# An attention and two-layer kernel: the second layer's low weight bits by ScalarE, one softmax moved, eight constant products fewer

## The chip, the cores and the metric

The kernel runs on one core of one Trainium2 chip. The metric is the device time of one launch in microseconds (us). TensorE (PE in the profile) multiplies matrices into PSUM, VectorE (DVE), ScalarE (ACT) and GpSimd (POOL) work on vectors, and SyncE (SP) issues the transfers. Each engine runs its own instructions in the order in which they were issued to it, and waits on semaphores for the others.

## The reference

Windowed attention is followed by two matrix products with an activation between them:

```python
# q, k, v: (8, 8, 576, 64); w_in (512, 2048) and w_out (2048, 512) are float64
scores = scale * np.matmul(q, k.transpose(0, 1, 3, 2))
# heads 0-3: the last 32 positions; heads 4-7: every 4th of the last 128
scores = np.where(masks[None, :, :, :], scores, -1000000000.0)
attn = np.exp(scores - np.max(scores, axis=-1, keepdims=True))
attn = attn / (np.sum(attn, axis=-1, keepdims=True) + 1e-09)
x = np.matmul(attn, v)           # then (4608, 512): tokens by heads
h = x @ w_in
g = np.where(h >= 1, h, np.where(h <= -1, 0.0, (h + 1) ** 2 / 4.0))
return (g @ w_out).astype(np.float32)
```

## The kernel before

Attention of 8 batches of 8 heads yields 9 blocks of 512 tokens. The two layers go through 9 x 16 steps (t, f): block t of tokens, chunk f of 128 hidden channels. In step s TensorE runs `layer1` of step s (12 products, tiles `h`, L404), then `layer2` of step s - 2 (12 products into the four banks `acc`, L440). Pieces of attention of later heads are hung between these halves by `place` and `run(u)`: scores (`s`, L208), transposes (`t`, L331), products with the values (`o`, L366). TensorE's order is the order of the code, written out by hand, and so is SyncE's. The order on VectorE, ScalarE and GpSimd is set by a scheduler from the dependences, from the place in the code, from `high_priority` and from `issue_after`, which puts what is issued inside it behind a given instruction.

Exact products need each float32 operand in two parts, a rounded copy and its remainder. After `layer1`, L418 clamps `h` (DVE), L421 squares (ACT), L423 takes the maximum (DVE), L424 writes the rounded copy `gh` (ACT), and L427 the remainder `gl` (DVE). `layer2` needs both. `h` has two PSUM banks, so `layer1` of step s also waits for `gh` and `gl` of step s - 2.

The weights come as float64 words, 32 chunks: `wi0` to `wi15`, `wo0` to `wo15`. `weights` turns one into two parts: L116 scales the high word into `m` (ACT, three buffers for all chunks), the top three bits of the low word are cut out (for `wi` by a byte read and a scaled copy on ACT, L122; for `wo` by a shift on DVE, L124), L127 merges both (DVE), L132 writes the rounded copy (ACT), L133 the remainder (POOL). `layer1` and `layer2` wait for L133. Chunks wo0 and wi3 are prepared ahead of step 0, then wo s and wi s + 3 from step s on, behind a mark of step s - 2.

The second batch's heads 8 to 15 run during the first steps. `scores_pair` masks the scores and takes row maxima on DVE (L182, tile `c8` for head 8). `softmax` for heads 8, 9, 10, 12 and 14 is done in one piece (`whole`): POOL subtracts the maximum (L297), ACT takes the exponential of the tile (L298), DVE sums the rows (L299); head 11 takes six exponentials (L256). Then ACT adds a small constant (L290), DVE inverts (L291), POOL multiplies (L292). Only then may TensorE transpose `c8` (tiles `t8_0`, `t8_4`), which stands between `layer2` of step 0 and `layer1` of step 3; `t9` follows that `layer1`, then come `layer2` of step 1, the values product `o8`, step 4, `t10`. All the `s`, `t` and `o` tiles take turns in two PSUM banks (`att`), so `t10_0` waits until the first half of `o8` has been copied out (L350 on ACT, L351 on DVE), and `t10_4` until the second half has.

`spin` issues products of a constant that nothing uses: 14 of them stand ahead of `layer1` of step 2.

Of the kernel before, what the change touches and what calls it, by code (L numbers as in the profile page):

```python
# [26 lines left out]
U8 = mybir.dt.uint8  # L27
AF = mybir.ActivationFunctionType
ALU = mybir.AluOpType

B, H, S, D = 8, 8, 576, 64
# [14 lines left out]
def body(ctx, tc, q, k, q2, k2, v, mask, eye, w_in, w_out, out):  # L46
    nc = tc.nc
# [22 lines left out]
    def load_pair(n):  # L70

        if 0 < n < H:
            qr, kr = borrow(f"qr{n}")[:, :S], borrow(f"kr{n}")[:, :KPAD]
        else:
            tags = ("qs", "kk") if n % 4 else ("qr", "kr")
            qr = pool.tile([128, S], F32, tag=tags[0], name=f"qr{n}")
            kr = pool.tile([128, KPAD + 32], F32, tag=tags[1], name=f"kr{n}")[:, :KPAD]
        nc.sync.dma_start(out=qr, in_=q[n // 2])
        nc.sync.dma_start(out=kr, in_=k[n // 2])
        for j in range(2):  # L80
            r = slice(64 * j, 64 * j + 64)
            heads[n + j] = dict(qs=qr[r], ks=kr[r])
# [18 lines left out]
    wi, wo, raws = {}, {}, {}  # L101
# [7 lines left out]
    def weights(f, w, name):  # L109

        raw = raws.pop((name, f))
        words = raw.rearrange("p (n x) -> p n x", x=2)
        low, high = words[:, :, 0], words[:, :, 1]
        m = pool.tile([128, DM], U32, tag="m", name=f"{name}_m{f}", bufs=3)

        nc.scalar.activation(  # L116
            out=m.bitcast(F32), in_=high.bitcast(F32), func=AF.Prelu, scale=2.0**-112, alpha=2.0**32
        )
        if name == "wi":

            top = raw.bitcast(U8).rearrange("p (n x) -> p n x", x=8)[:, :, 3]
            nc.scalar.activation(out=low, in_=top, func=AF.Copy, scale=1.0 / 32, bias=-31.0 / 64)  # L122
        else:
            nc.vector.tensor_scalar(  # L124
                out=low, in0=low, scalar1=29, scalar2=None, op0=ALU.logical_shift_right
            )
        nc.vector.scalar_tensor_tensor(  # L127
            out=m, in0=m, scalar=3, in1=low, op0=ALU.logical_shift_left, op1=ALU.bitwise_or
        )
        mf = m.bitcast(F32)  # L130
        w[f] = pool.tile([128, 2, DM], F32R, tag=f"{name}{f}", name=f"{name}{f}")
        nc.scalar.copy(out=w[f][:, 0], in_=mf)  # L132
        nc.gpsimd.tensor_tensor(out=w[f][:, 1], in0=mf, in1=w[f][:, 0].bitcast(F32), op=ALU.subtract)  # L133
# [27 lines left out]
    def spin(times, bank):  # L161

        half = half_t.broadcast_to([128, 128])
        for _ in range(times):
            PE.matmul(out=bank[:, :128], lhsT=half, rhs=half, start=True, stop=True)  # L165
# [117 lines left out]
    def softmax(n):  # L283
        c, st = heads[n]["c"], heads[n]["st"]
        if n in (8, 9, 10, 12, 14):
            whole(n)
        else:
            for t in range(NQ):
                exp(n, t)
        nc.scalar.activation(out=st[:, 1], in_=st[:, 1], func=AF.Copy, bias=EPS)  # L290
        nc.vector.reciprocal(out=st[:, 2], in_=st[:, 1])  # L291
        nc.gpsimd.tensor_tensor(out=c, in0=c, in1=spread(st[:, 2]), op=ALU.mult)  # L292
# [43 lines left out]
    last = {}  # L336
    xt = {}

    def xtile(t):
        if t not in xt:  # L340
            xt[t] = (
                pool.tile([128, NC, TOK], F32R, tag="xh", name=f"xh{t}", bufs=3),
                pool.tile([128, NC, TOK], F32R, tag="xl", name=f"xl{t}", bufs=3),
            )
        return xt[t]
# [51 lines left out]
    def layer1(t, f, cs=range(NC), bank=("h", 2)):  # L397
        xh, xl = xtile(t)
        if cs[0] == 0 and (t, f) not in hps:
            hps[t, f] = ps.tile([128, TOK], F32, tag=bank[0], name=f"h{t}_{f}", bufs=bank[1])  # L400
        hp = hps[t, f]
        terms = [(w, x, c) for c in cs for w, x in ((0, xh), (1, xh), (0, xl))]
        for i, (w, x, c) in enumerate(terms):
            PE.matmul(  # L404
                out=hp,
                lhsT=wi[f][:, w, 128 * c : 128 * c + 128],
                rhs=x[:, c],
                start=c == 0 and i == 0,
                stop=c == NC - 1 and i == len(terms) - 1,
            )  # L410
        if cs[-1] < NC - 1:
            return
        del hps[t, f]
        y = pool.tile([128, TOK], F32, tag="y", name=f"y{t}_{f}")
        gh = pool.tile([128, TOK], F32R, tag="gh", name=f"gh{t}_{f}", bufs=2)
        gl = pool.tile([128, TOK], F32R, tag="gl", name=f"gl{t}_{f}", bufs=2)
        with tc.high_priority(offset=60):
            nc.vector.tensor_scalar(  # L418
                out=y, in0=hp, scalar1=-1.0, scalar2=1.0, op0=ALU.max, op1=ALU.min
            )  # L420
            nc.scalar.activation(out=y, in_=y, func=AF.Square, bias=half_t, scale=0.5)  # L421

            activated = nc.vector.tensor_tensor(out=hp, in0=hp, in1=y, op=ALU.max)  # L423
            copied = nc.scalar.copy(out=gh, in_=hp)  # L424
            if t == 0:
                last["g", f] = copied, activated
            nc.vector.tensor_tensor(out=gl, in0=hp, in1=gh.bitcast(F32), op=ALU.subtract)  # L427
        gs[t, f] = gh, gl

    acc = {}  # L430
# [31 lines left out]
    def after_pair(n):  # L462
        softmax(n)
        softmax(n + 1)
        if n + 4 < native:
            load_pair(n + 4)
        elif n + 4 == native:
            load(native)
        else:
            split(native)  # L470
            load(native + 1)
# [70 lines left out]
    def early_values(n):  # L542
        with tc.high_priority(offset=150):
            values(n)
# [14 lines left out]
    with tc.manual_schedule(engines={mybir.EngineType.PE, mybir.EngineType.SP}):  # L559
        pair(0)  # L560
        pair(2)
        pair(4)
        pair(6)
        hps[0, 0] = ps.tile([128, TOK], F32, tag="h", name="h0_0", bufs=2)
        early_transposes(0)
        load_values(8)
        fetch(1, w_out, "wo")
        fetch(4, w_in, "wi")
        load_pair(10)
        fetch(2, w_out, "wo")  # L570
        fetch(5, w_in, "wi")
        fetch(3, w_out, "wo")
        for f in range(6, 9):
            fetch(f, w_in, "wi")
            fetch(f - 2, w_out, "wo")
        early_values(0)
        early_transposes(2)
        early_values(2)
        first = marks()
        spin(10, hps[0, 0])  # L580
        early_transposes(4)
        spin(3, hps[0, 0])
        early_transposes(6)
        behind(first, ("wi", 0), ("wi", 1))
        early_values(4)
        second = marks()
        layer1(0, 0, range(2))
        early_values(6)
        third = marks()
        behind(second, ("wi", 2))  # L590
        layer1(0, 1, range(2))
        scores_pair(H, 0, 4)
        scores_pair(H, 4, NQ)
        for f in range(9, 14):
            fetch(f, w_in, "wi")
            fetch(f - 2, w_out, "wo")
        with tc.issue_after(third[0].ins), tc.issue_after(third[1].ins):
            after_pair(H)
        behind(third, ("wo", 0), ("wi", 3))
        l2 = 0  # L600
        steps = [(t, f) for t in range(NT) for f in range(NF)]
        lag = 2
        for s in range(len(steps) + lag):
            if s == 3:
                for f, src, name in ((12, w_out, "wo"), (13, w_out, "wo"), (14, w_in, "wi")):
                    fetch(f, src, name)
                for f, src, name in ((14, w_out, "wo"), (15, w_in, "wi"), (15, w_out, "wo")):
                    fetch(f, src, name)
            if 0 < s < NF:
                todo = [("wo", s)]  # L610
                if s + 3 < NF:
                    todo.append(("wi", s + 3))
                behind(last["g", max(s - 2, 0)], *todo)
            if s == 2:
                acc[0] = ps.tile([128, DM], F32, tag="acc0", name="acc0_0")
                spin(14, acc[0])
            if s < 2:
                layer1(*steps[s], range(2, NC))
            elif s < len(steps):
                layer1(*steps[s])  # L620
            run(2 * s)
            while l2 <= s - lag and l2 < len(steps):
                layer2(*steps[l2])
                l2 += 1
            run(2 * s + 1)
        assert not slots
# [63 lines left out]
```

## Time and profile before

| | us |
|---|---|
| median of 3 runs | 925.8 (925.31 to 926.72) |
| the profiled execution | 924.65 |
| its span in the trace | 922.9 |
| PE, DVE, ACT, POOL busy | 905.3, 683.9, 487.3, 239.8 |

The profiled execution is 1.75 us longer than its span and 1.15 us below the median. Times in rows of the timeline are from the span's start. A row gives start, length, engine, line, operation, the tile written and the tiles read with buffer numbers left out, and in brackets how long the engine had idled and which instruction ended that. TensorE's float32 products are recorded as two instructions where operands are float32, so that 14 constant products are 28 rows.

### The profile page before, as it was taken

The page shows a single profiled execution, that of the slowest core. Times are in us where ns is not written, and L with a number is a line of the kernel's source. Part 1 is how long each engine was busy: PE and PEld are TensorE (multiplying, and loading weights), DVE is VectorE, ACT ScalarE, POOL GpSimd, SP SyncE. Part 2 cuts the span into 40 slices and gives each one's busy share as a digit, 9 for nine tenths or more (in the row PEclk, how much of TensorE's full clock was granted, in tenths as well). Part 3 has the DMA queues.
Part 4 walks back from the last instruction along what each step waited for, and adds up shares of the span by engine and source line. Part 5 has one row for each costly group of instructions (what it writes and reads, how often), then busy time and mean ns, then how long its engine had stood idle before and what let it go on. Part 6 is the DMA issues. An engine that isn't in the chain of part 4 may idle for free.

```text
span 922.9 us, 14426 instructions
## 1 busy us (share of the span) xinstructions
PE 905.3 (98%) x4886; PEld 742.5 (80%) x4886; DVE 683.9 (74%) x1982; ACT 487.3 (53%) x1336; POOL 239.8 (26%) x155
## 2 busy tenths in 40 slices
PE   7889999999999999999999999999999999999998
PEld 6677788888888888888888888888888888888886
DVE  6898898888888888788887888888888643334333
ACT  6778865555555556555555665555555322222222
POOL 4566453222223222222222322222222000000000
PEclk9999999999999999999999999999999999999999
DMA  9981003221232223112322223222321010001001
GB/s 350 407 311 45 1 27 103 84 58 57 70 116 71 70 71 107 51 57 69 116 71 71 71 61 103 67 70 71 116 71 44 1 46 1 1 1 47 0 1 47
DMA packets 31018, 73.87 MB, mean 80 GB/s; under 512 B 3520, under 2 KB 3808, under 8 KB 30944
## 3 DMA queue, kind: packets, MB, share of 16 engines
q1 hardware_dynamic: 30944, 72.94, 24.4%
q8 instruction: 39, 0.64, 0.3%
q14 instruction: 35, 0.29, 0.1%
HBM read 63.49 MB, written 9.44 MB: 79 GB/s over the span
## 4 chain that ended last, share of the span: by engine, by line
PE 91%; DMA 3%; DVE 3%; ACT 2%; issue 1%; POOL 1%; DVEq 0%; POOLq 0%; SPq 0%; ACTq 0%
PE acc L440 42%; PE h L404 40%; PE s L231 4%; PE o L366 3%; DMA wi_raw<-w_in 3%; ACT c L256 1%; DVE c L182 1%; PE s L165 0%; PE t L331 0%; DVE wi_m L127 0%; DVE c L299 0%; DVE wo_m L127 0%; POOL c L292 0%; PE s L208 0%; DVE wo_raw L124 0%
## 5 line engine op out<-in xcount | busy, mean ns | idle before, releaser
L440 PE MATMUL acc<-wo,gh 128*128 128x512 f32 x1152 | 382.8, 393 | 0.0
L404 PE MATMUL h<-xh,wi 128*128 128x512 f32 x1152 | 357.0, 391 | 0.9 <-DVE gl L427 0.9
L440 PEld LDWEIGHTS acc<-wo,gh 128*128 128x128 f32 x1152 | 216.5, 188 | 47.4
L404 PEld LDWEIGHTS h<-xh,wi 128*128 128x128 f32 x1152 | 209.1, 188 | 39.2 <-DVE gl L427 1.1
L440 PE MATMUL acc<-wo,gl 128*128 128x512 f32 x576 | 225.2, 391 | 0.0
L404 PE MATMUL h<-xl,wi 128*128 128x512 f32 x576 | 224.2, 389 | 0.0
L144 POOL TENSOR_TENSOR kk<-kr,kk 128x608 fp32r<-128x608 f32 x48 | 94.8, 1976 | 413.6 <-ACT kk L140 413.6
L256 ACT ACTIVATE c<-c 96x128 f32<-96x128 f32 x330 | 128.8, 391 | 118.1 <-DVE c L182 118.1
L421 ACT ACTIVATE y<-y,consts 128x512 f32<-128x512 f32 x144 | 104.2, 724 | 120.0 <-DVE y L418 119.9
L424 ACT CAST gh<-h 128x512 fp32r<-128x512 f32 x144 | 84.6, 587 | 124.4 <-PE acc L440 120.5
L418 DVE TENSOR_SCALAR y<-h 128x512 f32<-128x512 f32 x144 | 99.2, 689 | 56.5 <-PE h L404 56.1
L423 DVE TENSOR_TENSOR h<-h,y 128x512 f32<-128x512 f32 x144 | 100.6, 699 | 49.8 <-ACT y L421 48.3
L404 PEld LDWEIGHTS h<-xl,wi 128*128 128x128 f32 x576 | 108.2, 188 | 23.1
L427 DVE TENSOR_TENSOR gl<-h,gh 128x512 fp32r<-128x512 f32 x144 | 98.5, 684 | 37.1 <-ACT gh L424 37.0
L440 PEld LDWEIGHTS acc<-wo,gl 128*128 128x128 f32 x576 | 108.2, 188 | 19.5
L307 DVE STREAM_TRANSPOSE pt<-c 32x192 f32<-32x192 f32 x288 | 106.0, 368 | 6.4 <-POOL c L292 3.1
L250 DVE TENSOR_TENSOR c<-s,msk 96x256 f32<-96x256 f32 (+1 forms) x168 | 61.4, 377 | 36.3 <-PE s L231 35.3
L292 POOL TENSOR_TENSOR c<-c 96x768 f32<-96x768 f32 x56 | 83.0, 1484 | 16.4 <-DVE c L291 15.9
L182 DVE CUSTOM_DVE_ANT_0 c<-s,c 96x128 f32<-96x128 f32 x288 | 70.6, 281 | 1.0
L256 ACT ACTIVATION_READ_ACCUMULATOR c<-c 96x1 f32 x330 | 61.6, 187 | 0.0
L350 ACT CAST xh<-o 128x288 fp32r<-128x288 f32 (+8 forms) x112 | 38.7, 384 | 38.6 <-PE o L366 23.8
L231 PEld LDWEIGHTS s<-kk,qs 128*96 128x96 f32 x288 | 46.4, 161 | 15.5
(57 smaller groups left out, 645.2 us busy)
## 6 DMA issues: line engine op xcount, KB each, us to landing
kr<-k_in SPq DMA_DIRECT2D x56, 304.0 KB, 3.3
qr<-q_in SPq DMA_DIRECT2D x56, 288.0 KB, 2.8
vt<-v_in SPq DMA_DIRECT2D x32, 384.0 KB, 4.0
out<-out SPq DMA_DIRECT2D x36, 256.0 KB, 3.1
wi_raw<-w_in SPq DMA_DIRECT2D x16, 512.0 KB, 9.2
wo_raw<-w_in SPq DMA_DIRECT2D x16, 512.0 KB, 9.6
msk<-mask_in SPq DMA_DIRECT2D x1, 144.0 KB, 3.4
ident<-eye_in SPq DMA_DIRECT2D x1, 36.0 KB, 4.6
```

The lines of the kernel that those rows point to most:

```text
L144: nc.gpsimd.tensor_tensor(out=kk[:, 1], in0=hd["kr"], in1=kk[:, 0].bitcast(F32), op=ALU.subtract)
L231: PE.matmul(out=sv[:, t - t0], lhsT=hd["qs"][:, t * QT : (t + 1) * QT], rhs=hd["ks"][:, :, t * QT : t * QT + 128], start=True, stop=True,)
L256: last["act"] = nc.scalar.activation(out=c[:, t], in_=c[:, t], func=AF.Exp, bias=st[:, 0, t : t + 1], scale=-1.0, accum_out=st[:, 1, t : t ...
L292: nc.gpsimd.tensor_tensor(out=c, in0=c, in1=spread(st[:, 2]), op=ALU.mult)
L307: nc.vector.transpose(out=pt[r : r + 32, :, 32 * g : 32 * g + 32], in_=c[32 * g : 32 * g + 32, :, r : r + 32],)
L404: PE.matmul(out=hp, lhsT=wi[f][:, w, 128 * c : 128 * c + 128], rhs=x[:, c], start=c == 0 and i == 0, stop=c == NC - 1 and i == len(terms) - 1,
L418: nc.vector.tensor_scalar(out=y, in0=hp, scalar1=-1.0, scalar2=1.0, op0=ALU.max, op1=ALU.min)
L421: nc.scalar.activation(out=y, in_=y, func=AF.Square, bias=half_t, scale=0.5)
L423: activated = nc.vector.tensor_tensor(out=hp, in0=hp, in1=y, op=ALU.max)
L424: copied = nc.scalar.copy(out=gh, in_=hp)
L427: nc.vector.tensor_tensor(out=gl, in0=hp, in1=gh.bitcast(F32), op=ALU.subtract)
L440: PE.matmul(out=acc[m], lhsT=g[:, r], rhs=wo[f][:, w], start=f == 0 and i == 0, stop=f == NF - 1 and i == len(terms) - 1,)
```

## The change

It does three things. The byte read on ScalarE serves all 32 chunks, and the 16 shifts on VectorE are gone. `after_pair(H)`, which issues the softmax of heads 8 and 9 and the loads of head 12, stood ahead of step 0's weights; now it is issued inside step 0, behind the rounded copy `gh` of step 0. And `spin` ahead of step 2 makes 6 products, not 14.

```diff
-        if name == "wi":
-
-            top = raw.bitcast(U8).rearrange("p (n x) -> p n x", x=8)[:, :, 3]
-            nc.scalar.activation(out=low, in_=top, func=AF.Copy, scale=1.0 / 32, bias=-31.0 / 64)
-        else:
-            nc.vector.tensor_scalar(
-                out=low, in0=low, scalar1=29, scalar2=None, op0=ALU.logical_shift_right
-            )
+        top = raw.bitcast(U8).rearrange("p (n x) -> p n x", x=8)[:, :, 3]
+        nc.scalar.activation(out=low, in_=top, func=AF.Copy, scale=1.0 / 32, bias=-31.0 / 64)
...
-        with tc.issue_after(third[0].ins), tc.issue_after(third[1].ins):
-            after_pair(H)
         behind(third, ("wo", 0), ("wi", 3))
...
-                spin(14, acc[0])
+                spin(6, acc[0])
             if s < 2:
                 layer1(*steps[s], range(2, NC))
+                if s == 0:
+                    with tc.issue_after(last["g", 0][0].ins):
+                        after_pair(H)
```

TensorE's order changes only in the number of constant products, SyncE's not at all. The scheduler gives the other three engines a new order, which is shown at three places. Changed lines lie four to six numbers lower in the new kernel (L122 is L120 there, L298 is L292, L290 is L284, L292 is L286, L132 is L126, L133 is L127, L424 is L418, L350 is L344).

ScalarE before, from the exponential of head 8 to the small constant added to its sums. `gh0_0` is step 0's rounded copy, `wo_m1` and `wo_raw1` are `m` and the raw words of chunk wo1:

```order
L298 ACTIVATE c8_555<-c8_555 96x768
L256 ACTIVATE c11_651<-c11_651 96x128 x4
L298 ACTIVATE c9_557<-c9_557 96x768
L424 CAST gh0_0_642<-h0_0_306 128x512
L116 ACTIVATE wo_m1_669<-wo_raw1_334 128x512
L116 ACTIVATE wi_m4_676<-wi_raw4_336 128x512
L122 ACTIVATE wi_raw4_336<-wi_raw4_336 128x512
L116 ACTIVATE wo_m2_726<-wo_raw2_342 128x512
L122 ACTIVATE wi_raw5_344<-wi_raw5_344 128x512
L290 ACTIVATE c8_555<-c8_555 96x6
```

ScalarE in the new kernel, the twelve rows up to the same small constant; the exponential of head 8 (L292) stands right ahead of them, and ahead of that `gh0_0`:

```order
L116 ACTIVATE wo_m1_669<-wo_raw1_334 128x512
L120 ACTIVATE wo_raw1_334<-wo_raw1_334 128x512
L116 ACTIVATE wi_m4_676<-wi_raw4_336 128x512
L120 ACTIVATE wi_raw4_336<-wi_raw4_336 128x512
L116 ACTIVATE wo_m2_726<-wo_raw2_342 128x512
L120 ACTIVATE wo_raw2_342<-wo_raw2_342 128x512
L120 ACTIVATE wi_raw5_344<-wi_raw5_344 128x512
L292 ACTIVATE c9_557<-c9_557 96x768
L415 ACTIVATE y0_1_689<-y0_1_689,consts_66 128x512
L250 ACTIVATE c11_651<-c11_651 96x128 x2
L292 ACTIVATE c10_649<-c10_649 96x768
L284 ACTIVATE c8_555<-c8_555 96x6
```

Head 8's exponential now stands behind `gh0_0`, and between it and the constant there are seven weight operations, not five, and the exponentials of heads 9, 10 and 11 and step 1's square as well.

GpSimd before, from the subtraction for head 10 to the remainder of wi5. Between them stand the products with the inverted sums (L292) for heads 8, 9, 11 and 10:

```order
L297 TENSOR_TENSOR c10_649<-c10_649 96x768
L292 TENSOR_TENSOR c8_555<-c8_555 96x768
L133 TENSOR_TENSOR wo1_673<-wo_m1_669,wo1_673 128x512
L292 TENSOR_TENSOR c9_557<-c9_557 96x768
L133 TENSOR_TENSOR wi4_680<-wi_m4_676,wi4_680 128x512
L133 TENSOR_TENSOR wo2_730<-wo_m2_726,wo2_730 128x512
L292 TENSOR_TENSOR c11_651<-c11_651 96x768
L292 TENSOR_TENSOR c10_649<-c10_649 96x768
L133 TENSOR_TENSOR wi5_737<-wi_m5_733,wi5_737 128x512
```

And in the new kernel, the same stretch:

```order
L291 TENSOR_TENSOR c10_649<-c10_649 96x768
L127 TENSOR_TENSOR wo1_673<-wo_m1_669,wo1_673 128x512
L127 TENSOR_TENSOR wi4_680<-wi_m4_676,wi4_680 128x512
L286 TENSOR_TENSOR c8_555<-c8_555 96x768
L127 TENSOR_TENSOR wo2_730<-wo_m2_726,wo2_730 128x512
L286 TENSOR_TENSOR c9_557<-c9_557 96x768
L286 TENSOR_TENSOR c11_651<-c11_651 96x768
L286 TENSOR_TENSOR c10_649<-c10_649 96x768
L127 TENSOR_TENSOR wi5_737<-wi_m5_733,wi5_737 128x512
```

The product for head 8 went behind the remainders of wo1 and wi4, the one for head 9 behind that of wo2.

ScalarE before, in step 3, from `gh0_3` to the last copy out of the values product of heads 8 and 9 (`o8_0` and `o8_1`):

```order
L424 CAST gh0_3_841<-h0_3_827 128x512
L122 ACTIVATE wi_raw8_356<-wi_raw8_356 128x512
L350 CAST xh1_380<-o8_0_870 128x288
L116 ACTIVATE wo_m4_894<-wo_raw4_350 128x512
L350 CAST xh1_380<-o8_1_879 128x160
L116 ACTIVATE wi_m7_901<-wi_raw7_352 128x512
L132 CAST wo4_898<-wo_m4_894 128x512
L350 CAST xh2_888<-o8_1_879 128x128
```

And in the new kernel, the same stretch:

```order
L418 CAST gh0_3_833<-h0_3_819 128x512
L120 ACTIVATE wo_raw5_354<-wo_raw5_354 128x512
L120 ACTIVATE wi_raw8_356<-wi_raw8_356 128x512
L344 CAST xh1_380<-o8_0_862 128x288
L116 ACTIVATE wo_m5_953<-wo_raw5_354 128x512
L126 CAST wi7_897<-wi_m7_893 128x512
L344 CAST xh1_380<-o8_1_871 128x160
L116 ACTIVATE wi_m8_960<-wi_raw8_356 128x512
L126 CAST wo5_957<-wo_m5_953 128x512
L344 CAST xh2_880<-o8_1_871 128x128
```

There `wo_m4`, `wi_m7` and the rounded copy of wo4 stand ahead of `gh0_3`, and wo5, wi7, wi8 stand between the copies out of `o8`.

## Prediction

> **What bounds the kernel now.** I read the page first, then the chain that ended last, then the waits of TensorE, then the timeline of each engine from 40 to 75 us.
>
> ```profile
> PE 905.3 (98%) x4886; PEld 742.5 (80%) x4886; DVE 683.9 (74%) x1982; ACT 487.3 (53%) x1336; POOL 239.8 (26%) x155
> PE 91%; DMA 3%; DVE 3%; ACT 2%; issue 1%; POOL 1%; DVEq 0%; POOLq 0%; SPq 0%; ACTq 0%
> ```
>
> TensorE is busy for 98% of the span and carries 91% of the chain. So only what TensorE waits for, or multiplies for nothing, can be gained, and every new wait on it is paid in full. Its timeline shows where that is, near the places that the change touches:
>
> ```profile
> 45.51 4.73 PE L165 MATMUL acc<-consts 128*128 128x128 f32 x28
> 49.99 0.70 PE L404 MATMUL h<-xh,wi 128*128 128x512 f32 x2
> 55.57 0.66 PE L331 MATMUL t<-ident,c 96*128 96x96 f32 x6
> 57.10 0.73 PE L404 MATMUL h<-xh,wi 128*128 128x512 f32 x2 [0.88 <-DVE gl L427]
> 65.21 1.37 PE L366 MATMUL o<-pt,vt 128*64 128x96 f32 x24 [1.77 <-DVE pt L334]
> 69.63 0.52 PE L331 MATMUL t<-ident,c 96*128 96x96 f32 x4
> 71.56 0.35 PE L331 MATMUL t<-ident,c 96*128 96x96 f32 x2 [1.41 <-DVE xl L351]
> 98.10 0.71 PE L331 MATMUL t<-ident,c 96*128 96x96 f32 x6 [0.26 <-POOL c L292]
> ```
>
> In order: the 14 constant products, step 2, transpose `t8` of head 8, step 3 (0.88 us of waiting for `gl0_1`), `o8` (1.77), `t10_0`, `t10_4` (1.41), `t12`. From 71.7 us on almost nothing is waited for:
>
> ```profile
> core 0: us, PE busy (x) PEld busy (x) DVE busy (x) ACT busy (x) POOL busy (x), PEclk, DMA share, GB/s
> 50.00:57.10 7.10, 6.22 (x33) 5.00 (x31) 7.10 (x12) 6.12 (x18) 5.02 (x4) 1.00 1.04 407
> 57.10:65.20 8.10, 6.33 (x30) 4.90 (x30) 8.07 (x10) 4.65 (x10) 6.82 (x6) 1.00 0.70 249
> 71.60:98.00 26.40, 26.25 (x152) 20.65 (x152) 23.52 (x57) 22.43 (x51) 17.66 (x13) 1.00 0.12 40
> ```
>
> TensorE is busy 26.25 of 26.40 us there, so when `t10_4` starts (71.56 now) decides the time: what it is shifted by, the end is shifted by. Before that, VectorE is the full engine (7.10 of 7.10, 8.07 of 8.10) and ScalarE is at 6.12 of 7.10: neither has room.
>
> **The byte read for wo.** Sixteen shifts leave VectorE, sixteen byte reads come to ScalarE.
>
> ```profile
> L124 DVE TENSOR_SCALAR wo_raw<-wo_raw x16: 411/646/3201, 37.5 to 134.5; 128x512 uint32<-128x512 uint32 x16
> L122 ACT ACTIVATE wi_raw<-wi_raw x16: 642/668/694, 27.4 to 118.8; 128x512 uint32<-128x512 uint8 x16
> L127 DVE SCALAR_TENSOR_TENSOR wo_m<-wo_m,wo_raw x16: 672/687/2595, 38.5 to 136.3; 128x512 uint32<-128x512 uint32 x16
> 52.05 2.81 DVE L124 TENSOR_SCALAR wo_raw<-wo_raw 128x512 uint32<-128x512 uint32 x1
> 51.62 1.71 POOL L292 TENSOR_TENSOR c<-c 96x768 f32<-96x768 f32 x1 [2.32 <-DVE c L291]
> 53.29 1.29 POOL L133 TENSOR_TENSOR wo<-wo_m,wo 128x512 fp32r<-128x512 f32 x1
> 61.70 2.60 DVE L127 SCALAR_TENSOR_TENSOR wo_m<-wo_m,wo_raw 128x512 uint32<-128x512 uint32 x1
> 65.08 1.77 DVE L127 SCALAR_TENSOR_TENSOR wi_m<-wi_m,wi_raw 128x512 uint32<-128x512 uint32 x1
> 65.02 1.28 POOL L133 TENSOR_TENSOR wo<-wo_m,wo 128x512 fp32r<-128x512 f32 x1 [1.28 <-ACT wo L132]
> ```
>
> (The first three rows give min/median/max in ns.) The shift of 0.41 us took 2.81 at 52.05: it ended at 54.86, just after GpSimd's two instructions end at 54.58. The merge L127, 0.69 us in the median, took 1.77 because GpSimd held on until 66.30. So these two wait out GpSimd; a byte read never does (0.64 to 0.69). VectorE gets back 16 x 0.41 = 6.6 us at least, and more where a shift waited; ScalarE pays 0.56 us each, the spacing of its queue. After 71.6 us both have slack (23.52 and 22.43 of 26.40), and I cost those chunks at nothing; without that slack, ten chunks would add 5.6 us to ScalarE. The four reads for wo0 to wo3 fall into the full stretch and count below. The merges stay on VectorE and keep waiting.
>
> [...]
>
> **Six constant products.** Rows of what surrounds them:
>
> ```profile
> 41.52:44.93 3.41, 1.86 (x11) 1.09 (x10) 3.41 (x26) 1.79 (x4) 3.41 (x3) 1.00 1.00 398
> 44.93:48.34 3.41, 3.41 (x19) 3.13 (x16) 3.41 (x14) 3.41 (x12) 0.83 (x2) 0.50 1.04 410
> 62.00:65.40 3.40, 1.62 (x10) 1.02 (x9) 3.40 (x4) 1.47 (x4) 2.12 (x3) 1.00 0.90 349
> 42.23 0.68 DVE L418 TENSOR_SCALAR y<-h 128x512 f32<-128x512 f32 x1
> 44.52 0.69 DVE L423 TENSOR_TENSOR h<-h,y 128x512 f32<-128x512 f32 x1
> 48.96 0.67 DVE L427 TENSOR_TENSOR gl<-h,gh 128x512 fp32r<-128x512 f32 x1
> ```
>
> After a stretch with 1.55 us of idling (41.52 to 44.93) the granted clock is 0.50 for 3.41 us. The rows at 45.51 and 49.99 give 4.48 us for 14 products: by the 3.41 us at half clock about 0.38 us each there, 0.25 after. Step 2 waits for `gl0_0`, done at 49.63, so the products hid that wait, and eight fewer gain only if `gl0_0` comes earlier. It does: the shifts of wo1 and wo2 and the sums of heads 8 and 9 leave VectorE's queue ahead of it. Against that, wi3's merge now stands behind eight row maxima, where GpSimd works on wo0, whose rounded copy is one byte read later: 0 to 0.6 us, and I take 0.6, as in the row at 65.08. So the maximum L423 ends at 45.7; then clamp 0.6, four row maxima 0.85, `gl0_0` until 47.9. Six products from 46.1 end at about 48.3. Step 2 starts at 48.2, 1.8 us earlier, and TensorE is at `t8` at 55.57 - 1.8 = 53.8.
>
> **The moved softmax.** `t8` needs head 8's inverted sums multiplied in.
>
> ```profile
> 43.86 0.84 ACT L298 ACTIVATE c<-c 96x768 f32<-96x768 f32 x1 [0.19 <-POOL c L297]
> 44.61 0.39 ACT L256 ACTIVATE c<-c 96x128 f32<-96x128 f32 x1
> 48.46 0.66 ACT L122 ACTIVATE wi_raw<-wi_raw 128x512 uint32<-128x512 uint8 x1
> 49.02 0.66 ACT L116 ACTIVATE wo_m<-wo_raw 128x512 f32<-128x512 f32 x1
> 50.14 0.19 ACT L290 ACTIVATE c<-c 96x6 f32<-96x6 f32 x1
> 50.23 0.71 ACT L421 ACTIVATE y<-y,consts 128x512 f32<-128x512 f32 x1
> 67.55 0.59 ACT L424 CAST gh<-h 128x512 fp32r<-128x512 f32 x1
> 68.60 0.39 ACT L350 CAST xh<-o 128x288 fp32r<-128x288 f32 x1
> 54.88 0.91 DVE L299 TENSOR_REDUCE c<-c 96x6 f32<-96x768 f32 x1
> 58.97 3.53 POOL L292 TENSOR_TENSOR c<-c 96x768 f32<-96x768 f32 x2
> 67.58 1.37 POOL L133 TENSOR_TENSOR wi<-wi_m,wi 128x512 fp32r<-128x512 f32 x1 [1.28 <-ACT wi L132]
> ```
>
> Now the exponential runs at 43.86, the constant is added at 50.14, and GpSimd multiplies from 51.62 to 53.33, 2.2 us before TensorE asks. In the new order ScalarE has the four exponentials of head 11 until 46.1, `gh0_0` until 46.6, then head 8's exponential (0.74 of queue) until 47.3. Seven weight operations (7 x 0.56 = 3.9) bring it to 51.2, head 9's exponential to 52.0, the square to 52.6, two exponentials of 0.39 to 53.4, head 10's to 54.1: the constant at 54.1, where it was at 50.14. On VectorE the sums of head 10 (0.91) stand ahead of the inverse, which comes at 55.3. On GpSimd the remainders of wo1 and wi4 stand ahead: their rounded copies follow the constant on ScalarE (54.2 to 55.3), so 54.9 to 57.4; the product then ends at 58.9. `t8` starts at 58.9, not 55.57 (+3.3), and TensorE idles 5.1 us from 53.8.
>
> Step 3 follows at 59.4, not 57.10 (+2.3), since its own 0.88 us for `gl0_1` lies inside. `t9` waits for head 9's product behind wo2's remainder (58.9 + 1.25 + 1.46 + a merge let in = 62.2): just when TensorE gets there. `o8` comes at 66.7, not 65.21 (+1.5); its 1.77 us of waiting has been used up.
>
> Then `t10`. GpSimd has ten instructions in a row from 54.9 to the end of wi6's remainder: 6 x 1.25 + 4 x 1.46 = 13.3 us, and 0.6 for each merge let in, up to three: 68.2 to 70.1, where it now ends at 67.58 + 1.37 = 68.95. On ScalarE `gh0_3` now stands behind wo4's and wi7's scaling, which need the buffers of wi5 and wo3 from GpSimd (65.7 to 67.7, 67.0 to 69.0), and behind the rounded copy of wo4, whose merge waits for GpSimd in turn. So `gh0_3` at 68.5 to 71.5 (67.55 now); two byte reads (1.1); the first copy out of `o8` at 70.1 to 73.1 (68.60 now); then wo5, wi7, the second copy, wi8, wo5 again, the last copy 2.6 us later, and its remainder on VectorE behind wi8's merge (0.6, or 2.2 behind GpSimd). `t10_4` starts between 74.1 and 78.1, now 71.56: +2.5 if no merge waits, +6.6 if each waits as in the row at 61.70. In the stretch now each second merge waits, and the two products at 58.97 took 3.53, not 2.9; I take a value nearer the upper end, +5.2.
>
> The loads of head 12 keep their place in SyncE's queue, and cost nothing; loads of late weights that wait for the tiles of heads 8 and 9 start some 3 us later and land long before step 12.
>
> **The clock.** TensorE idles for 5.1 us ahead of `t8` and for most of 70.8 to 76.8 around `t10`. The first stretch's half clock falls on step 3, and `t10`'s wait hides it. The second falls on full work: between 0 (1.8 us of idling in 62.00 to 65.40 left it at 1.00) and 3.41 us at half clock (1.7), or a window and a quarter (2.1). I take +0.8.
>
> [...]
>
> **Sum.** +5.2 + 0.8 = +6.0 on the profiled execution's 924.65 gives 930.65; the median lies 1.15 above that execution, so 931.8.
>
> **The rivals.** *It becomes faster.* Without a late `t8`, step 3 would still start no earlier than 57.1, since `gl0_1` comes at 57.2 (`gh0_1` stands behind three rounded copies); but the waits of 1.77 and 1.41 could go with the shifts' 2.81 and its like: 925.8 - 3.2 = 922.6. It decides at head 8's product ending by 55.6, so the constant by about 51; the row at 50.14 shows that this needs the old order. *Nothing changes:* -1.8 at step 2 is eaten by `gl0_1`, and the two waits stay: 925.8. *Late but caught up:* `t8` late, merges unhindered, no half clock: +2.5, 928.3. For it speaks that ten instructions cost GpSimd no more than now; against it the two rows at 61.70 and 65.08. *Everything waits:* +6.6 + 2.1 = +8.7, 934.5; it needs a halved clock, for which the two idle stretches speak.
>
> **How the numbers follow.** Forecast (929.5 to 934.5) 0.62, late but caught up (927.7 to 929.5) 0.18, above 934.5 0.08, no change 0.05, faster 0.07. A measurement tells 0.2%, 1.85 us, from no change: slower 0.88, same 0.05, faster 0.07. The range 927.8 to 934.8 leaves out the last two and a part of the third.
>
> **What would show it.** Right: in the new profile `t8` waits some 5 us for GpSimd's product of `c`, `t10` some 5 us in two parts for the copies out of `o8` on VectorE and ScalarE, the row of the constant for head 8 stands near 54, and the granted clock drops once or twice between 55 and 83 us. Wrong: a `t8` wait under 2 us, or a merge L127 never above 1.3 us.

## The result, and the profile after

| | median, us | range | ratio to before, with its interval |
|---|---|---|---|
| before | 925.55 | 924.96 to 926.72 | |
| after | 931.03 | 930.86 to 931.67 | 1.0058 [1.0046, 1.0071] |

The changed kernel is slower, by 5.5 us. Its profiled execution took 930.96 us, with a span of 929.0, where the one before took 924.65 and 922.9: 6.3 and 6.1 us. The row of the engines after:

```profile
PE 907.1 (98%) x4870; PEld 743.2 (80%) x4870; DVE 672.3 (72%) x1966; ACT 494.1 (53%) x1352; POOL 240.5 (26%) x155
```

VectorE has 16 instructions and 11.6 us less, ScalarE 16 and 6.8 us more, TensorE 16 records (8 constant products) less and yet 1.8 us more of busy time: a window at half clock is recorded as busy in full (3.41 of 3.41 us in 59.29:62.70 below). None of these numbers tells the loss. The timeline does. TensorE's rows of the kernel after, at the places where the prediction showed those of before:

```profile
40.30 1.12 PE L202 MATMUL s<-kr,qr 64*96 64x128 f32 x16
46.46 2.82 PE L159 MATMUL acc<-consts 128*128 128x128 f32 x12
49.04 0.71 PE L398 MATMUL h<-xh,wi 128*128 128x512 f32 x2
59.12 1.11 PE L325 MATMUL t<-ident,c 96*128 96x96 f32 x6 [4.34 <-POOL c L286]
59.94 1.20 PE L398 MATMUL h<-xh,wi 128*128 128x512 f32 x2
65.17 0.69 PE L325 MATMUL t<-ident,c 96*128 96x96 f32 x6 [0.96 <-DVE pt L328]
68.58 1.21 PE L360 MATMUL o<-pt,vt 128*64 128x96 f32 x24
73.46 0.52 PE L325 MATMUL t<-ident,c 96*128 96x96 f32 x4 [0.68 <-DVE xl L345]
75.76 0.39 PE L325 MATMUL t<-ident,c 96*128 96x96 f32 x2 [1.78 <-ACT pt L328]
103.97 0.71 PE L325 MATMUL t<-ident,c 96*128 96x96 f32 x6 [0.30 <-POOL c L286]
```

One row of the kernel before has to stand beside the first:

```profile
39.94 1.12 PE L208 MATMUL s<-kr,qr 64*96 64x128 f32 x16
```

These 16 score products are the last place that the change cannot reach. They started 0.36 us later after, because that execution lost 0.34 us in its first 5 us (its opening constant products took 4.50 us, not 4.16). So starts are compared from this row on. `t8` moved from 15.63 to 18.82 (+3.19), `t10_4` from 31.62 to 35.46 (+3.84), `t12` from 58.16 to 63.67 (+5.51), the end from 882.96 to 888.70 (+5.74). The loss is therefore 3.84 us up to `t10_4`, 1.67 between `t10_4` and `t12`, 0.23 in all that follows.

The 1.67 is the clock. The windows after; columns: length, TensorE's busy time, weight load, VectorE, ScalarE, GpSimd, each with its instructions, then the granted clock, DMA:

```profile
55.87:59.29 3.42, 0.17 (x2) 0.17 (x3) 1.73 (x6) 3.42 (x10) 3.42 (x4) 1.00 0.59 238
59.29:62.70 3.41, 3.41 (x13) 2.83 (x13) 3.41 (x3) 3.41 (x7) 3.41 (x3) 0.50 0.38 101
72.94:76.35 3.41, 1.11 (x8) 0.92 (x9) 3.12 (x7) 3.41 (x9) 2.38 (x2) 1.00 0.01 5
76.35:79.77 3.42, 3.42 (x10) 2.64 (x9) 0.80 (x2) 0.49 (x1) 1.84 (x2) 0.50 0.00 0
```

Two windows in which TensorE mostly stood (busy for 0.17 us at `t8`, and for 1.11 at `t10`) are each followed by 3.41 us at half clock. The first falls on step 3, the second on full work: ten records where the window 72.24:75.65 before, at full clock, holds twenty (its row stands in the last section).

And the chain that makes `t10` late, on ScalarE (exponential and constant of head 8, `gh0_3`, the first and last copy out of `o8`, the copy of `t10_0`), on VectorE (the merges of wi5, wo3, wi6, the last remainder out of `o8`) and on GpSimd (the products of head 8, then of heads 9, 11 and 10):

```profile
46.85 0.84 ACT L292 ACTIVATE c<-c 96x768 f32<-96x768 f32 x1
54.36 0.19 ACT L284 ACTIVATE c<-c 96x6 f32<-96x6 f32 x1
70.82 0.58 ACT L418 CAST gh<-h 128x512 fp32r<-128x512 f32 x1
72.42 0.40 ACT L344 CAST xh<-o 128x288 fp32r<-128x288 f32 x1
75.03 0.30 ACT L344 CAST xh<-o 128x128 fp32r<-128x128 f32 x1
75.19 0.51 ACT L328 COPY pt<-t 128x384 f32<-128x384 f32 x1
59.24 1.62 DVE L121 SCALAR_TENSOR_TENSOR wi_m<-wi_m,wi_raw 128x512 uint32<-128x512 uint32 x1
60.78 3.38 DVE L121 SCALAR_TENSOR_TENSOR wo_m<-wo_m,wo_raw 128x512 uint32<-128x512 uint32 x1
64.95 2.33 DVE L121 SCALAR_TENSOR_TENSOR wi_m<-wi_m,wi_raw 128x512 uint32<-128x512 uint32 x1
75.72 0.28 DVE L345 TENSOR_TENSOR xl<-o,xh 128x128 fp32r<-128x128 f32 x1
57.60 1.46 POOL L286 TENSOR_TENSOR c<-c 96x768 f32<-96x768 f32 x1
60.27 5.22 POOL L286 TENSOR_TENSOR c<-c 96x768 f32<-96x768 f32 x3
```

The constant comes 7.5 us after the exponential, GpSimd's product behind it ends at 59.06, and `t8` starts then. The three merges, 0.69 us each in the median of all chunks, took 7.33 together while GpSimd worked. But they took 6.06 before, and the last of them, wi6's, ended at the same place: 26.98 us behind the start of the 16 score products, 26.91 before. What came late stands behind it. Step 3's clamp before, then step 3's clamp and the rounded copy of wo4 after:

```profile
64.21 0.68 DVE L418 TENSOR_SCALAR y<-h 128x512 f32<-128x512 f32 x1
```

```profile
67.21 0.68 DVE L412 TENSOR_SCALAR y<-h 128x512 f32<-128x512 f32 x1
70.30 0.62 ACT L126 CAST wo<-wo_m 128x512 fp32r<-128x512 f32 x1 [0.20 <-DVE wo_m L121]
```

Before, the clamp stood ahead of wi6's merge (65.08); in the new order it stands behind it, and step 3's products themselves ended only at 64.21 (60.14 before). So ScalarE still had wi6's rounded copy, a copy of `t9`, step 3's square, two scalings and wo4's rounded copy to do between that merge and `gh0_3`: 3.54 us, 0.70 before. That is 2.84 of the 3.84 us. One more byte read ahead of the first copy out of `o8` adds 0.55, the longer queue between the copies 0.37.

### The profile page after: what moved, and what is told of

Same layout as the page of the kernel before. It is cut to its first block, busy times and chain, and to the rows that moved or that the text cites. A ratio compares the mean times of both kernels' runs of the same rounds, so it can differ in the third digit from the quotient of the medians.

```text
span 929.0 us, 14399 instructions
## 1 busy us (share of the span) xinstructions
PE 907.1 (98%) x4870; PEld 743.2 (80%) x4870; DVE 672.3 (72%) x1966; ACT 494.1 (53%) x1352; POOL 240.5 (26%) x155
## 4 chain that ended last, share of the span: by engine, by line
PE 89%; ACT 3%; DVE 2%; issue 2%; POOL 2%; DMA 1%; DVEq 0%; POOLq 0%; ACTq 0%
PE acc L434 41%; PE h L398 40%; PE s L225 4%; PE o L360 3%; ACT c L250 1%; DVE c L176 1%; POOL wi L127 1%; PE s L159 0%; POOL wo L127 0%; DMA vt<-v_in 0%; PE t L325 0%; DVE c L293 0%; DVE xl L345 0%; ACT wi_raw L120 0%; ACT wo_raw L120 0%
## 5 line engine op out<-in xcount | busy, mean ns | idle before, releaser
L418 ACT CAST gh<-h 128x512 fp32r<-128x512 f32 x144 | 84.3, 586 | 126.1 <-PE acc L434 122.3
L286 POOL TENSOR_TENSOR c<-c 96x768 f32<-96x768 f32 x56 | 83.4, 1491 | 10.8 <-DVE c L285 10.8
L344 ACT CAST xh<-o 128x288 fp32r<-128x288 f32 (+8 forms) x112 | 38.6, 383 | 37.8 <-PE o L360 22.5
```

## The experiments

Each variant was timed beside the kernel before on the same chip. This table has the start of three tiles in each profiled execution, counted from the start of the 16 score products, the two stretches behind them (`t10_4` to `t12`, and `t12` to the end of the span), and the time of the merges of wi5, wo3 and wi6 together:

| kernel | `t8` | `o8` | `t10_4` | to `t12` | to the end | merges |
|---|---|---|---|---|---|---|
| before | 15.63 | 25.27 | 31.62 | 26.54 | 824.80 | 6.06 |
| after | 18.82 | 28.28 | 35.46 | 28.21 | 825.03 | 7.33 |
| e1, bytes only | 16.12 | 24.88 | 30.61 | 26.77 | 825.19 | 4.69 |
| e2, move and six products | 17.42 | 28.08 | 33.38 | 26.57 | 824.80 | 6.91 |
| e3, six products only | 15.39 | 25.32 | 31.67 | 28.12 | 824.78 | 6.05 |
| e4, after with 14 products | 18.86 | 27.15 | 35.36 | 28.94 | 824.98 | 6.11 |
| e5, constants of 8 to 11 on VectorE | 14.58 | 27.70 | 33.98 | 26.60 | 824.74 | 4.15 |
| e6, TensorE kept busy at `t10` | 18.85 | 28.31 | 35.88 | 26.60 | 825.10 | 7.31 |
| e7, bytes for wo0 to wo3 | 18.87 | 29.55 | 36.04 | 26.59 | 825.31 | 7.37 |
| e8, bytes for wo4 to wo15 | 17.37 | 26.91 | 32.61 | 26.64 | 824.94 | 4.22 |
| e9, constants of 8 and 9 on VectorE | 14.43 | 24.02 | 31.18 | 26.60 | 825.53 | 5.11 |
| e10, e8 and e9 together | 13.87 | 22.50 | 31.81 | 28.50 | 824.71 | 6.96 |
| e11, before with late bytes | 15.68 | 23.41 | 32.73 | 28.01 | 824.82 | 6.35 |
| e12, e1 again | 16.17 | 24.89 | 30.65 | 26.76 | 825.17 | 4.69 |

The last stretch is the same within some 0.8 us everywhere. `t10_4` to `t12` has two values, 26.5 to 26.8 and 28.0 to 28.9; the second belongs to those five executions in which a half-clock window falls behind `t10_4`. So the start of `t10_4` and the clock behind it make nearly all of every difference of over 1 us, as the prediction's sum assumed. The time of the merges does not go with it: e4 has 6.11 us of merges, as before, and the loss of the kernel after.

TensorE's order is fixed by the code, but an edit to what the other three engines do lets the scheduler write a new order for them. So a variant can differ from its neighbour in more places than its edit names. In the traces only e3 has the order of the kernel that it was made from; e4 and e6 differ at a few places, the others at more.

**e1 and e12: the byte read alone.**

```diff
-        if name == "wi":
...
-        else:
-            nc.vector.tensor_scalar(
-                out=low, in0=low, scalar1=29, scalar2=None, op0=ALU.logical_shift_right
-            )
```

> The byte reads alone: softmax of heads 8 and 9 at its old place, 14 constant products, no shift on VectorE. Theory A (ScalarE's queue and the merges that wait for GpSimd set the end): t8 waits under 0.5 us, but four more byte reads stand ahead of the copies out of o8 on ScalarE, so t10_4 comes 2.5 to 4 us later than before; 928.3 to 929.8 us. Rival B (the moved softmax is the whole loss, the byte reads relieve the full VectorE): the waits ahead of o8 and t10_4 shrink, 922.5 to 925.5 us.

Measured: 925.27 (924.93 to 926.4) beside 926.01, ratio 0.9993 [0.9983, 1.0002]. That lies in the rival's range and not in the 928.3 to 929.8 of theory A. The waits ahead of `o8` and `t10_4` shrank, as the rival had it, to 0.63 and 1.21 us, but `t8` came 0.49 us later. With the softmax in its old place the reads cost nothing:

```profile
52.20 0.20 ACT L284 ACTIVATE c<-c 96x6 f32<-96x6 f32 x1
53.47 1.47 POOL L286 TENSOR_TENSOR c<-c 96x768 f32<-96x768 f32 x1 [3.59 <-DVE c L285]
56.85 0.66 PE L325 MATMUL t<-ident,c 96*128 96x96 f32 x6
```

The constant of head 8 is late by the reads, but its product still ends at 54.94, 1.9 us before TensorE asks.

> The kernel before with the byte read for all sixteen wo chunks, as in the first comparison (ratio 0.9993, 0.9983 to 1.0002), in more rounds, beside the others of this call. If the byte read alone is a gain: 925.0 to 925.6, with an interval of the ratio below 1. If not: within 0.3 us of the kernel before.

Measured: 925.39 (924.49 to 926.3) beside 925.32, ratio 0.9999 [0.9990, 1.0008]. So it is no gain either. `t10_4` is a whole microsecond earlier in both executions (30.61 and 30.65 for 31.62), and 0.2 and 0.4 us of that are given back in the two stretches behind it; that the rest does not show in the medians is not explained by these traces.

**e2: the move and the six products, with the shifts left on VectorE.**

```diff
-        with tc.issue_after(third[0].ins), tc.issue_after(third[1].ins):
-            after_pair(H)
...
-                spin(14, acc[0])
+                spin(6, acc[0])
...
+                if s == 0:
+                    with tc.issue_after(last["g", 0][0].ins):
+                        after_pair(H)
```

> The moved softmax with 6 constant products; the wo shifts stay on VectorE. Theory A: head 8's added constant still stands behind head 10's exponential on ScalarE, t8 comes near 57.3 us (1.7 later than before, a wait of 3 to 4 us), and t10_4 3 to 5 us later: 928.5 to 931 us. Rival B: nearly the whole loss, 930 to 931.5 us. Rival C (the byte reads are the loss): 925 to 926 us.

Measured: 927.59 (926.68 to 929.82), ratio 1.0021 [1.0012, 1.0031]: slower, but by 1.6 us, below the ranges that expected a loss and above the one that expected none.

```profile
58.37 0.71 PE L331 MATMUL t<-ident,c 96*128 96x96 f32 x6 [2.90 <-POOL c L292]
74.33 0.39 PE L331 MATMUL t<-ident,c 96*128 96x96 f32 x2 [0.76 <-ACT pt L334]
```

`t8` waits here too, 2.90 us for 4.34, and `t10_4` is 1.76 us late, not 3.84. The parts do not add: -0.7 (e1) and +1.6 make +5.5 together.

**e3 and e4: the constant products.** In the kernel before:

```diff
-                spin(14, acc[0])
+                spin(6, acc[0])
```

> The kernel before with 6 constant products, nothing else. Theory A: step 2 waits for the remainder gl0_0 that VectorE ends at 49.6 us, so a wait of about 2 us takes the place of eight products: 925.5 us, within 0.6. Rival D (the products themselves cost): 923.3 to 924 us. If the clock misses them, step 2 runs at half clock: up to 927 us.

Measured: 926.56 (925.78 to 927.14), ratio 1.0005 [0.9996, 1.0014], a little above the expected range and not told from before. Step 2 started at 50.13 after a wait of 1.56 us for `gl0_0`: the wait took the products' place. And the kernel after with 14:

```diff
-                spin(6, acc[0])
+                spin(14, acc[0])
```

> The changed kernel with 14 constant products. Theory A: eight more end 2 us later, and the wait of 4.3 us ahead of t8 shrinks by as much: 931.0 us, within 0.6. Rival D: 933 us.

Measured: 931.62 (931.06 to 932.18), ratio 1.0060 [1.0045, 1.0075], at the upper edge of theory A's range. `t8` waited 2.56 us, 1.78 less, as theory A had it. The number of constant products explains none of the loss.

**e7 and e8: which byte reads.** Both change the kernel after:

```diff
-        top = raw.bitcast(U8).rearrange("p (n x) -> p n x", x=8)[:, :, 3]
-        nc.scalar.activation(out=low, in_=top, func=AF.Copy, scale=1.0 / 32, bias=-31.0 / 64)
+        if name == "wi" or f < 4:       # e8: f >= 4
...
+        else:
+            nc.vector.tensor_scalar(
+                out=low, in0=low, scalar1=29, scalar2=None, op0=ALU.logical_shift_right
+            )
```

> The kernel after, with the byte read for wo0 to wo3 alone; wo4 to wo15 get their low bits by the shift on VectorE as before. Theory (the four reads that stand in ScalarE's queue around the moved softmax make the difference between the move alone, 927.6, and all three parts, 931.0): 930.3 to 931.7, t8 waits over 4 us. Rival (the later reads, wo4 to wo9, which stand ahead of the copies out of o8, make it): 926.8 to 928.5, t8 still waits over 4 us.

> The kernel after, with the byte read for wo4 to wo15 alone; wo0 to wo3 get their low bits by the shift as before. Theory (the reads of wo0 to wo3 make the difference): as the move alone, 926.8 to 928.5, t8 waits near 2.9 us. Rival (the later reads make it): 930.0 to 931.5.

Measured: 930.62 (929.6 to 931.47), ratio 1.0056 [1.0039, 1.0073], for wo0 to wo3; 927.57 (927.1 to 928.84), ratio 1.0022 [1.0012, 1.0031], for wo4 to wo15. Both as the theory had it in time. The four early reads make the difference between the move alone and all three parts, the twelve later ones none. The waits at `t8` were not as expected: 2.96 us with the early reads, not over 4, and 3.53 with the late ones, not 2.9. With the early reads it still came as late as in the kernel after (18.87 for 18.82); TensorE only got there later, through two half-clock windows in a row ahead of it. The rows of the constant and of step 2's square, of the move alone (first, with the constants of heads 8 and 9 in one row) and of the early reads:

```profile
53.50 0.29 ACT L290 ACTIVATE c<-c 96x6 f32<-96x6 f32 x2
56.38 0.70 ACT L421 ACTIVATE y<-y,consts 128x512 f32<-128x512 f32 x1
```

```profile
53.95 0.20 ACT L289 ACTIVATE c<-c 96x6 f32<-96x6 f32 x1
57.39 0.71 ACT L420 ACTIVATE y<-y,consts 128x512 f32<-128x512 f32 x1
```

Counted from the 16 score products (40.95 and 39.86) the constants are at 12.55 and 14.09: 1.5 us later, of which two more reads ahead of it, 0.56 us of queue each, make 1.1; the rest is there already at `gh0_0`. The square is at 15.43 and 17.53, 2.1 us later, with three more reads ahead of it. VectorE's maximum waits for the square, and the merge of wi5 comes behind it: it starts at 17.67 and 20.36. These 2.7 us are the whole shift of `t10_4` (33.38 and 36.04). The merge of wo3 is no part of it: it takes 3.21 us in the move alone, too, and 3.38 with the early reads.

**e5 and e9: the constant's place.** The kernel after, with the constant added on VectorE:

```diff
-        nc.scalar.activation(out=st[:, 1], in_=st[:, 1], func=AF.Copy, bias=EPS)
+        if 8 <= n < 12:                 # e9: n in (8, 9)
+            nc.vector.tensor_scalar(out=st[:, 1], in0=st[:, 1], scalar1=EPS, scalar2=None, op0=ALU.add)
+        else:
+            nc.scalar.activation(out=st[:, 1], in_=st[:, 1], func=AF.Copy, bias=EPS)
```

> The kernel after, with the small constant of heads 8 to 11 added on VectorE in place of ScalarE. Theory (the constant stands in ScalarE's queue behind seven weight operations and three exponentials, and that makes t8 late, and with it GpSimd's run and t10): t8 starts near 54 without a wait over 1 us, t10_4 near 72 to 73, 925.0 to 927.5. Rival (the stretch is full anyway, VectorE and GpSimd set t10, and the late t8 lies inside that): t8 comes early but t10_4 stays near 75.5, 929.5 to 931.5.

Measured: 929.08 (928.52 to 930.26), ratio 1.0038 [1.0023, 1.0053]: between the two. `t8` came early, as the theory had it, and yet only 2 us of the loss went.

```profile
57.91 2.50 DVE L285 TENSOR_SCALAR c<-c 96x6 f32<-96x6 f32 x1
60.55 0.65 DVE L424 TENSOR_TENSOR gl<-h,gh 128x512 fp32r<-128x512 f32 x1
61.25 0.83 PE L401 MATMUL h<-xh,wi 128*128 128x512 f32 x2 [4.63 <-DVE gl L424]
```

The constant of head 10, six numbers a row, waited 2.50 us on VectorE and ended at 60.41, when GpSimd had finished the product that it was in and the remainder of wo1 behind it (60.38). `gl0_1` is queued behind it, and step 3 waited 4.63 us for `gl0_1`: the wait went from `t8` to step 3. The next variant leaves heads 10 and 11 on ScalarE:

> The kernel after, with the small constant of heads 8 and 9 alone added on VectorE; heads 10 and 11 keep theirs on ScalarE. Theory (with the constants of heads 8 to 11 on VectorE, 929.1, t8 came early, but head 10's constant waited 2.50 us there for GpSimd, ahead of gl0_1, and step 3 paid for it: the gain was turned into a new wait): t8 without a wait, step 3 waits under 3 us, t10_4 some 2 to 3 us earlier than with four heads, 925.5 to 927.5. Rival (the merges behind GpSimd set t10, wherever the constant is added): 928.2 to 930.5.

Measured: 925.91 (925.08 to 926.69) beside 925.32, ratio 1.0006 [0.9997, 1.0016]. The loss is gone.

```profile
50.47 0.17 DVE L285 TENSOR_SCALAR c<-c 96x6 f32<-96x6 f32 x1
51.01 1.89 POOL L289 TENSOR_TENSOR c<-c 96x768 f32<-96x768 f32 x1 [1.39 <-DVE c L288]
58.22 0.74 PE L401 MATMUL h<-xh,wi 128*128 128x512 f32 x2 [2.05 <-DVE gl L424]
67.28 0.39 ACT L347 CAST xh<-o 128x288 fp32r<-128x288 f32 x1
68.13 0.58 ACT L421 CAST gh<-h 128x512 fp32r<-128x512 f32 x1
72.27 0.39 PE L328 MATMUL t<-ident,c 96*128 96x96 f32 x2 [2.65 <-ACT pt L331]
```

The constant at 50.47 stands two places behind head 8's sum; the product of head 8 ends at 52.90, and `t8` (14.43) waits for nothing. Step 3's clamp (63.52) stands ahead of wi6's merge (64.98) again, and ScalarE makes the first copy out of `o8` ahead of `gh0_3`, not 1.6 us behind it. All three parts of the change are in this kernel, so their loss is not bound to them. Which part of the gain is the constant's own place, and which the new order that came with it, these runs do not separate.

**e6: the clock.** The kernel after, with five constant products between `t10_0` and `t10_4`:

```diff
             for t in range(t0, t1):
                 PE.transpose(tp[:, QT * (t - t0) : QT * (t - t0 + 1)], c[:, t], ident)
+            if n == 10 and t0 == 0:
+                spin(5, tp[:, 384:])
```

> The kernel after, with five constant products between t10_0 and t10_4, into columns of t10_0's bank that nothing reads, so that TensorE doesn't idle while it waits for the copy of t10_0. Theory (1.7 us of the loss is the half clock in the window after the idling at t10): the half-clock window near 76 to 80 is gone, t10_4 stays where it is, 929.0 to 930.0. Rival (the waits alone make the loss, the half clock falls on time that is waited for anyway): 930.5 to 931.5.

Measured: 930.51 (929.6 to 930.72), ratio 1.0050 [1.0035, 1.0065], at the rival's edge. The profiled execution is the one of 929.6 us, and in it the half-clock window behind `t10` is gone:

```profile
76.03:79.45 3.42, 3.42 (x21) 2.87 (x21) 0.76 (x2) 0.94 (x3) 2.01 (x2) 1.00 0.00 0
```

`t10_4` to `t12` takes 26.60 us there, not 28.21, while `t10_4` itself came 0.4 us later. So the 1.67 us are the clock, in that execution. The other three took 930.35 to 930.72, and whether they kept the clock no trace shows; by the medians the products are worth half a microsecond, which the intervals do not tell from nothing.

**e10 and e11: two tries for more.** e10 joins e8 and e9 (their two edits above); e11 is the kernel before with the byte read from wo4 on:

```diff
-        if name == "wi":
+        if name == "wi" or f >= 4:
```

> The kernel after, with the byte read for wo4 to wo15 alone and the constant of heads 8 and 9 on VectorE: both causes taken away at once, the move and the six products kept. Theory (the reads of wo0 to wo3 and the late constant are what the move cost, and nothing else): 924.3 to 926.5, below or at the kernel before. Rival (the move costs by its place, whatever stands on ScalarE): as with the late reads alone, 926.8 to 928.5.

> The kernel before, with the byte read for wo4 to wo15 alone; the softmax stays where it was and there are 14 products. Theory (the late reads are hidden and free VectorE): as the byte read for all in the old place, 924.8 to 925.7. Rival (they do nothing, or ScalarE pays for them at the copies out of o8): 925.8 to 927.0.

Measured: 927.46 (926.21 to 929.53), ratio 1.0025 [1.0014, 1.0036], and 927.94 (927.45 to 928.87), ratio 1.0033 [1.0021, 1.0046]. Both missed their theory; e10 lies in its rival's range, e11 above both of its ranges. e11 is 2.6 us slower than before, and e1 is not: in the old place the four early reads, which cost 3.2 us behind the moved softmax (e7 against e2, each from its own kernel before), bring 2.6 back. The rows of e11, with `gh0_3` and the first copy out of `o8`:

```profile
62.90 3.00 DVE L127 SCALAR_TENSOR_TENSOR wi_m<-wi_m,wi_raw 128x512 uint32<-128x512 uint32 x1
69.23 0.52 PE L331 MATMUL t<-ident,c 96*128 96x96 f32 x4 [1.58 <-DVE xl L351]
66.61 0.59 ACT L424 CAST gh<-h 128x512 fp32r<-128x512 f32 x1
68.20 0.38 ACT L350 CAST xh<-o 128x288 fp32r<-128x288 f32 x1
72.77 0.55 PE L331 MATMUL t<-ident,c 96*128 96x96 f32 x2 [3.02 <-DVE xl L351]
```

`o8` came 1.86 us earlier than before (23.41), and nothing was gained by it: the merge of wi6 took 3.00 us, the copies out of `o8` stand behind it, `t10` waited 4.6 us in two parts, and the half clock followed (28.01). e10 shows the same: `t8` at 13.87 and `o8` at 22.50, the earliest of all, then 2.65 and 1.59 us of waiting at `t10` and two half-clock windows in a row, which make 1.96 us; `t10_4` itself came 0.19 us late. So a punctual `t8` is not enough. What sets these two apart from e1, e12 and e9 is a place on ScalarE: in e1 and e9 the first copy out of `o8` stands ahead of `gh0_3` (25.65 and 26.51 us from the score products in e1, 26.19 and 27.04 in e9), in e10 and e11 behind it and two byte reads (28.33 behind 26.73, 28.16 behind 26.56). Why the scheduler orders them so is not known, and no run moves that copy alone, so this is not shown to be the cause. No variant beats the kernel before: e12 and e9 are level with it.

## Why the prediction was right

It said 931.8, slower; 931.03 was measured. By its steps:

- **The move makes `t8` late: right.** Constant at 54.1, measured 54.36; product at 58.9, measured 59.06; `t8` +3.3, measured +3.19; wait 5.1, measured 4.34, because step 2 came 1.3 us earlier, not 1.8. That a late `t8` makes the loss is in part argued: with the constant of heads 8 and 9 on VectorE the ratio fell from 1.0058 to 1.0006 (e9), but the scheduler changed the order elsewhere too, and in e10 the same edit made `t8` punctual and gained nothing against e8.
- **The early byte reads count, the later ones are free after 71.6 us: right** (e7, e8), in this order of the queues. For the order before, e11 shows that the later reads are not free: they cost 2.6 us there. That was not foreseen, nor that the early reads are worth having there and in e9: without them it is e10, 1.55 us slower.
- **The six products cost nothing: right** (e3, e4), and for the reasons given: in the kernel before, `gl0_0` takes their place; in the kernel after, what they save is waited for at `t8`.
- **`t9` at 62.2 and `o8` +1.5: too early.** (By the prediction's own rows, without the wait of 1.77 us and with step 3 at +2.3, `o8` would have been at +0.5.) `t9` came at 65.17, `o8` at +3.0. Step 3 ran at half clock from 59.29 to 62.70, and the copy of `t8` on VectorE stood behind the merge of 3.38 us. It cost nothing more: `t10_0` still waited 0.68 us for the copy out of `o8`.
- **GpSimd and ScalarE up to the copies: right in the times, in part for another reason.** Its run was to end at 68.2 to 70.1, the remainder of wi6 ended at 69.68; `gh0_3` 68.5 to 71.5, measured 70.82; first copy out of `o8` 70.1 to 73.1, measured 72.42; last copy 2.6 us later, measured 2.61. But the scalings of wo4 and wi7 did not wait for GpSimd's buffers, and wo4's merge was not held (0.68 us): `gh0_3` was late by the length of ScalarE's queue behind wi6's merge.
- **`t10_4` +5.2: the term that was mis-sized.** It measured +4.2 as the rows stand and +3.84 from the common row. The step that failed is the last one: `t10_4` was to wait for the last remainder out of `o8`, behind wi8's merge. That remainder ran from 75.72 to 76.00 and `t10_4` started at 75.76: it did not wait for it. In this order `t10_4` waits for ScalarE's copy of `t10_0` (75.19, 0.51 us), and so it seems to take the bank of `t10_0`; in the kernel before it waited for the remainder. wi8's merge took 0.84 us, not the 2.2 of the upper bound. From the start of the last copy to `t10_4` the prediction's two bounds leave 1.4 and 2.4 us; it was 0.73. The waits at `t10`, forecast as some 5 us in two parts, were 0.68 and 1.78, since TensorE itself got there later.
- **The clock +0.8: too small.** It was 1.67, one window of 3.41 us on full work, near the upper end of 0 to 2.1. The window and a quarter behind the 2.1 was the author's estimate, and no run shows it: half clock lasted 3.41 us, or in e4, e7, e8 and e10 two such windows in a row. The two errors, -1.4 and +0.9, nearly cancel; that the sum of +6.0 is so near the +5.74 from the common row is luck. The 1.15 us by which the median was to lie above the profiled execution did not come either: it was 0.07.
- **"Late but caught up"** would have needed merges of the median length; they took 7.33 us for 2.07. **"It becomes faster"** asked for head 8's product by 55.6, and said that this needs the old order. It does not: e9 has it at 52.90 with all three parts of the change. But the 922.6 did not come either; `t10_4` then waited 2.65 us for ScalarE's copy of `t10_0`, which stood behind weight operations.

## What to carry to other kernels

When three engines are full around a hand-off, a change that moves work between them is priced by what stands ahead of each small instruction on the path, not by the work moved: here a constant added to six numbers a row stood behind seven weight operations in one queue, and taking it to another engine, with the order that the scheduler then wrote, won 5 us back. Try that before undoing the change, but look at what stands behind it there: in e5 the same edit for heads 10 and 11 as well moved the wait to the next matmul, and in e10, with other byte reads, it won nothing. And parts of such a change are to be timed together, since apart they were worth -0.7 to +0.1 (bytes) and +1.6 (the move with the products), and together +5.5.

## What the runs showed of the hardware

The granted clock fell to 0.50 in windows of 3.41 us. Within an execution their starts lie whole windows apart (45.63, 59.29 and 76.35 us after: four and five windows). Counted from the 16 score products, the first came at 4.99 us before and at 5.33 after. Equal waiting cost a window in one execution and none in another. The same wait at `t10`, in the kernel before and in e3:

```profile
68.82:72.24 3.42, 1.90 (x12) 1.24 (x11) 3.13 (x8) 3.42 (x9) 1.36 (x2) 1.00 0.06 22
72.24:75.65 3.41, 3.41 (x20) 2.85 (x19) 2.95 (x7) 2.92 (x6) 3.08 (x3) 1.00 0.00 0
```

```profile
69.69:73.11 3.42, 1.90 (x12) 1.38 (x11) 3.30 (x7) 3.42 (x9) 1.67 (x2) 1.00 0.01 5
73.11:76.52 3.41, 3.41 (x9) 2.56 (x8) 2.11 (x5) 1.56 (x3) 3.00 (x2) 0.50 0.00 0
```

Both were busy for 1.90 of 3.42 us; one kept the clock, the other lost it for a window; what decided between them the profile does not show. In the fourteen traces, with windows laid from the first drop and looked at from 36 to 88 us, the thirteen full-clock windows busy for less than 1.45 us were each followed by half clock; of those between 1.48 and 1.95 some were and some were not; of those above 2.0 none was.

A VectorE instruction on 96 x 6 numbers took 2.50 us in e5, where it ended 0.03 us behind GpSimd's remainder of wo1 (60.38), and 0.17 in e9, where GpSimd ran nothing from 49.62 to 51.01. And the merge of 3.38 us after lasted 2.69 us longer than the median of 0.69, which is more than one of GpSimd's products takes (1.46), as was already so of the row of 2.60 us before (1.91 longer).
